# Sixteen value loads moved behind other casts in GpSimd's instruction stream

## The chip, the core and the metric

One NeuronCore of a Trainium2 chip runs the whole program. The engines named below are TensorE (PE in the profile, its weight loads PEld), VectorE (DVE), ScalarE (ACT), GpSimd (POOL) and SyncE (SP). The metric is the device time of one execution in microseconds (us). The kernel before takes 266.47 us, the median of five runs (266.29 to 267.04).

## What is computed

The first half is attention over 4 batches x 8 heads, 768 positions of 64 values. Each query sees only some blocks of 64 keys: its own block and the 3 blocks whose mean key scores best among those not in the future. The second half is a mixer over the 768 x 512 result: one product over positions, one over channels, each with a residual.

```python
k_rep = k.reshape(B, H, 12, 64, D).mean(axis=3)
gate  = where(causal, einsum('bhsd,bhnd->bhsn', q, k_rep), -1e9)
sel   = top 3 of gate, and the own block
attn  = softmax(where(mask(sel) & causal, q @ k.T / 8, -1e9))
x     = (attn @ v), heads side by side          # (4, 768, 512)
u     = x + (relu(x.T @ w_tok1) @ w_tok2).T     # w_tok1 768x256, w_tok2 256x768
out   = u + relu(u @ w_ch1) @ w_ch2             # w_ch1 512x1536, w_ch2 1536x512
```

Inputs and output are float32; the kernel computes most products in float16.

## The kernel before, in words

**Tiling.** Two heads of one batch are a pair, so there are 16 pairs, numbered 0 to 15, four for each batch. For a pair the kernel does the following. Words in brackets are the names that the profile shows.

- SyncE loads keys and queries as float32, two DMAs each (kl and ql, line 313). Three buffers each exist for kl and ql, so the load of pair i waits for the transposes of pair i-3.
- PE transposes them (tkl, tql, line 358) into one of two large PSUM buffers (ring "big"); ACT copies the result out to SBUF (kt, qt, line 367), which frees the PSUM buffer.
- GpSimd casts kt and qt to float16, one cast for each head (KA, QA, line 374): four casts for a pair. For pair 0 ACT does this instead (line 379).
- DVE sums the key blocks (kst, ks, lines 387 and 395), PE multiplies queries by these sums (gps, line 405), DVE picks the three best blocks (gm, m, bn, lines 447 to 483), PE turns the resulting bias (bps, line 493), and DVE puts it under the queries (QA, line 499), so that the score product adds the mask by itself. From pair 6 on, this gate is made for groups of two or four pairs (gtp, gbp, lines 415 and 435).
- PE makes the scores (sps, lines 513 and 517) in three parts for each head, each in a "big" buffer; ACT takes the exponential (e, line 526); DVE clears the half above the diagonal (line 533; for pair 0 PE does it).
- GpSimd issues the load of the pair's values (V, line 320), one DMA that reads float32 and writes float16. There are six V buffers, so the load of pair i waits for the attention product of pair i-6.
- PE multiplies exponentials and values (avp, line 545), and DVE divides by the sums (rc, x, lines 553 and 564).

When the pairs of a batch are done, the mixer of that batch follows: tok and ups (lines 607 and 621 for batch 0, 576 and 588 for the others), then the two large products (c, lines 657 and 678), and the stores. Their weights come through ten more DMAs that GpSimd issues: two for w (lines 706, 707) and eight for wc (lines 709, 711).

**What sets the order.** A planner (`plan`, line 109) runs when the program is built. It gets a list of operations, each with its engine, an assumed duration, a priority, the operations it depends on and the buffers it takes; for a DMA, `size` is the assumed time of its transfer. It puts each engine's operations in an order, and the kernel emits them in that order. On the chip each engine runs its own stream in order, and a semaphore wait exists only where data or a buffer demands one. A dependency that is given to the planner alone sets the place in the stream and nothing else. So for the value load of pair i the planner is told (line 832) to wait for the query transposes of pair 1, 2, 2, 3, 3, 4, 4, 5, ... ; on the chip the DMA waits for what stands ahead of it on GpSimd, and for its buffer.

The planner also fills time that it believes idle on PE up to 46 us with dummy matmuls (avp<-warm, line 695), 136 of them in this program.

GpSimd's stream before, from the end of its set-up to the first casts of pair 8 (V0 is the value load of pair 0; kt1 means both casts of the keys of pair 1, kt7a and kt7b the single ones; w1, w2, wcA to wcH the weight loads):

```
V0 kt1 qt1 V1 V2 kt2 qt2 kt3 V3 w1 w2 qt3 V4 wcA wcB kt4 V5 qt4 V6 wcC wcD own V7
kt5 qt5 wcE wcF kt6 V8 qt6 kt7a wcG wcH kt7b qt7 V9 V10 kt8 ...
```

Of the kernel before, what the change touches and what calls it, by code (L numbers as in the profile page):

```python
# [28 lines left out]
R = 5  # L29
# [10 lines left out]
def QACT(i):  # L40
    return i < 1


GATE = {2: 700, 3: 700, 4: 730}
GROUPED = [[0], [1], [2], [3], [4], [5], [6, 7], [8, 9, 10, 11], [12, 13, 14, 15]]
WAIT = [("kt", 3, 1), ("kt", 3, 1), ("qt", 3, 1), ("qt", 3, 1), ("qt", 4, 1), ("qt", 4, 1),
        ("qt", 5, 1), ("qt", 5, 1), ("qt", 6, 1), ("qt", 6, 1)]
# [171 lines left out]
def kernel(  # L219
# [71 lines left out]
    def op(eng, occ, rec, deps, prio, fn, takes=(), size=0):  # L291
        o = Op(eng, occ, rec, deps, prio, fn, takes, size)
        ops.append(o)
        return o

    def pe(occ, deps, prio, fn, takes=(), tail=170):
        return op("PE", occ, occ + tail, deps, prio, fn, takes)

    def act(cols, deps, prio, fn, takes=()):
        return op("ACT", 70 + cols * 0.833, 173 + cols * 0.833, deps, prio, fn, takes)  # L300

    def dve(occ, deps, prio, fn, takes=()):
        return op("DVE", occ, occ + 84, deps, prio, fn, takes)


    def load_qk(i, t32, src):
        b, h = pairs[i]

        def f():
            t = sb(t32, [128, NJ, 2 * D], FP, f"{t32}_{i}")  # L310
            T[t32, i] = t
            for g in range(2):
                nc.sync.dma_start(out=t[:, :, D * g:D * g + D], in_=src[b, h + g].rearrange("(j p) d -> p j d", p=128))  # L313
        return f

    def load_v(i):
        b, h = pairs[i]

        def f():
            nc.gpsimd.dma_start(out=V16[i % (R + 1)].rearrange("p g j d -> p (g j) d")[:, :, 0:D],  # L320
                                in_=v[b, h:h + 2].rearrange("g (j p) d -> p (g j) d", p=128))
        return f
# [29 lines left out]
    def transposes(t32, i):  # L352
        def f():
            p = ps("big", None, f"t{t32}")
            T["tr", t32, i] = p
            t = T[t32, i]
            for j in range(NJ):
                nc.tensor.transpose(out=p[:, 128 * j:128 * j + 128], in_=t[:, j, :], identity=ident32)  # L358
        return f

    def evac_t(t32, i):
        def f():
            name = "qt" if t32 == "ql" else "kt"
            t = sb(name, [128, S], FP, f"{name}_{i}")
            T[name, i] = t
            p = T["tr", t32, i]
            nc.scalar.copy(out=t, in_=p[:, 0:S])  # L367
        return f

    def cast(dst, name, i, x):  # L370
        def f():
            lo = 64 * x
            to, src = dst[i % R][x][0:64, :], T[name, i][lo:lo + 64, :]
            nc.gpsimd.tensor_copy(out=to, in_=src)  # L374
        return f

    def cast_act(dst, name, i, x):
        def f():
            nc.scalar.copy(out=dst[i % R][x][0:64, :], in_=T[name, i][64 * x:64 * x + 64, :])
        return f  # L380
# [115 lines left out]
    def put_mask(gi, s, x):  # L496
        def f():
            i = GROUPED[gi][s]
            nc.vector.tensor_copy(out=QA[i % R][x][64:MK, 128:S], in_=T["bps", gi][32 * s:32 * s + 2 * NB, :])  # L499
        return f  # L500
# [197 lines left out]
    O = {}  # L698
# [13 lines left out]
    W = []  # L712

    def prepare(i):
        b, h = pairs[i]
        gi = [n for n, G in enumerate(GROUPED) if i in G][0]
        i0 = GROUPED[gi][0]
        pre = 10.0 * (i0 - (AHEAD if i < FIRST else LATER)) + 2.5 * (i - i0) - (0 if len(GROUPED[gi]) == 1 else EXTRA)
        vpre = 10.0 * (i - (AHEAD if i < FIRST else LATER))
        old = i - R  # L720

        def last_scores(x):
            return [O.get(("sc", old, x, g)) for g in range(3)]

        for t32, src, off in (("kl", k, 0), ("ql", q, 0.1)):
            bf = Buf(t32)
            O[t32, i] = op("SP", 950, 0, [], pre - 12 + off, load_qk(i, t32, src), [bf], size=1750)
            big = Buf("big")
            O["tr", t32, i] = pe(660, [O[t32, i]], pre + off, transposes(t32, i), [big], tail=320)
            bf.users.append(O["tr", t32, i])  # L730
            name = "kt" if t32 == "kl" else "qt"
            tb = Buf(name)
            O[name, i] = act(768, [O["tr", t32, i]],
                             pre + 0.5 + off, evac_t(t32, i), [tb])
            big.users.append(O[name, i])
            dst = KA if name == "kt" else QA
            for x in range(2):
                occ = 770
                if QACT(i):
                    O["cast", name, i, x] = act(768, [O[name, i]] + last_scores(x), pre + 0.9 + 0.2 * x + off, cast_act(dst, name, i, x))  # L740
                    tb.users.append(O["cast", name, i, x])
                    continue
                O["cast", name, i, x] = op("POOL", occ, occ + 55, [O[name, i]] + last_scores(x), pre + 4 + off,
                                           cast(dst, name, i, x))
                tb.users.append(O["cast", name, i, x])
            if name == "kt":
                O["ksum", i] = dve(870, [O["kt", i]], pre + 1, ksum(i))
                tb.users.append(O["ksum", i])
                O["kcopy", i] = dve(200, [O["ksum", i], O.get(("gate", old))], pre + 1, kcopy(i))
            else:  # L750
                qb = tb
        O["v", i] = op("POOL", 1060, 0, [O.get(("av", i - R - 1, x)) for x in range(2)], vpre + 2, load_v(i), size=1350)
        n = len(GROUPED[gi])
        O["qb", i] = qb
        if i == GROUPED[gi][-1]:
            G = GROUPED[gi]
            if n == 1:
                gb = Buf("bank")
                O["gate", i] = gate_op = pe(1120, [O["kcopy", i], O["qt", i]], pre + 2, gate(i), [gb])
            else:  # L760
                tbig = Buf("big")
                gate_op = pe(GATE[n], [O["kcopy", m] for m in G] + [O["qt", m] for m in G], pre + 2, gate_t(gi), [tbig])
                for m in G:
                    O["gate", m] = gate_op
                gtb = Buf("gt")
                ge = act(S - 128, [gate_op], pre + 2.1, gate_e(gi), [gtb])
                tbig.users.append(ge)
                gb = Buf("big")
                gback = pe(550, [ge], pre + 2.2, gate_b(gi), [gb])
                gtb.users.append(gback)  # L770
            for m in G:
                O["qb", m].users.append(gate_op)
            gs = Buf("gs")
            O["gm", gi] = dve(75 + 125 * n, [gate_op] if n == 1 else [gback, own_op], pre + 3, gm(gi), [gs])
            gb.users.append(O["gm", gi])
            tops = [dve(720, [O["gm", gi]], pre + 3, top(gi, s)) if s == 0 else None for s in range(n)]
            for s in range(1, n):
                tops[s] = dve(720, [tops[0]], pre + 3, top(gi, s))
            O["lt", gi] = dve(75 + 125 * n, tops, pre + 3, below(gi))
            O["bias", gi] = dve((75 + 125 * n) if n == 4 else 200 * n, [O["lt", gi], O.get(("mask", gi - NBN))] + ([own_op] if n == 4 else []), pre + 3, bias(gi))  # L780
            gs.users += [O["bias", gi]]
            O["lt", gi].two = O["bias", gi].two = True
            mb = Buf("bank")
            O["mask", gi] = pe(280, [O["bias", gi]], pre + 4, mask(gi), [mb])
            for s, m in enumerate(G):
                for x in range(2):
                    O["put", m, x] = dve(410, [O["mask", gi]] + [O.get(("sc", m - R, x, g)) for g in range(3)],
                                         pre + 4, put_mask(gi, s, x))
                    mb.users.append(O["put", m, x])
# [38 lines left out]
        for i in G:  # L828
            attend(i)

    for i, d in enumerate((1, 2, 2, 3, 3, 4, 4, 5, 6, 7, 8, 9, 10, 11, 12, 13)):
        O["v", i].deps.append(O["tr", "ql", d])
    own_op.deps.append(O["cast", "qt", 4, 1])
    for x in range(2):
        O["cast", "kt", 0, x].deps.append(O["qt", 0])
    O["ksum", 1].deps.append(O["bias", 0])
    for n, (at, f) in enumerate(wq):
        W.append(op("POOL", 700, 0, [O[("cast",) + WAIT[n]]], at, f, size=4500 if n < 2 else 2100))

    for b in range(B):  # L840
        fill = 1000.0 * (b + 1)
# [5 lines left out]
        if b == 0:  # L847
            for c in range(4):
                bk = Buf("bank")
                at = fill + c  # L850
# [133 lines left out]
```

The softmax here doesn't subtract the row's maximum and nothing guards it: scores larger than these inputs give would overflow.

## Time and profile before

| what | us |
|---|---|
| median of five runs | 266.47 |
| the profiled execution, its own time | 266.29 |
| its span, first to last instruction | 264.2 |
| PE busy | 257.2 (97%) |
| DVE busy | 158.4 (60%) |
| ACT busy | 145.1 (55%) |
| GpSimd busy | 80.1 (30%) |

The span is what the profiler's instructions cover; the execution's own time is 2.1 us more. PE's busy time is modelled by the profiler and counts matmuls at half clock as busy. In the table of DMA issues the value loads have the time from issue to landing:

```profile
V<-in_v_dram POOLq DMA_DIRECT2D x16, 192.0 KB, 7.2
wc<-in_moe_w_ch_dram POOLq DMA_DIRECT2D x8, 384.0 KB, 9.8
w<-in_moe_w_tok_dram POOLq DMA_DIRECT2D x2, 384.0 KB, 9.6
```

The columns are the issuing queue, the number of issues, the size of one as written (the reads are twice that, float32), and the median us from issue to landing.

### The profile page before, as it was taken

To read this page: it belongs to the slowest core of one execution; us is meant where nothing else is said; L and a number is where in the kernel's file an instruction comes from. 1 tells how busy PE (TensorE), PEld (TensorE's weight loads), DVE (VectorE), ACT (ScalarE), POOL (GpSimd) and SP (SyncE) were. 2 spreads that over 40 slices of the span, in tenths; PEclk is the share of its full clock that TensorE was granted. 3 is DMA by queue.
4 is the path that set the end of the run, shared out by engine and by line. 5 is a ranking of instruction groups with operands and counts; after the bars stand their busy time and mean duration, and the time that the engine had idled before them with its cause. 6 is when DMAs were issued, how large, how long until landed. Compare 5 with 4: busy or idle time off the path is not lost.

```text
span 264.2 us, 5842 instructions
## 1 busy us (share of the span) xinstructions
PE 257.2 (97%) x2304; PEld 167.7 (63%) x2304; DVE 158.4 (60%) x536; ACT 145.1 (55%) x195; POOL 80.1 (30%) x112
## 2 busy tenths in 40 slices
PE   8989999999999999899999999999999999999994
PEld 7877788886768777455656666654455544465443
DVE  3576869986987669986548975483243253333222
ACT  2855898777788965549873699950034400044000
POOL 8393909849464944226420000000000000000000
PEclk9997999999999999999999999999999999999999
DMA  8999999999999999168511000009220025310032
GB/s 167 207 184 205 173 182 221 184 186 200 199 161 171 202 177 143 40 95 136 72 42 42 0 2 0 2 0 201 79 79 2 0 54 144 122 40 0 2 144 94
DMA packets 91322, 28.77 MB, mean 109 GB/s; under 512 B 84896, under 2 KB 87840, under 8 KB 91296
## 3 DMA queue, kind: packets, MB, share of 16 engines
q1 hardware_dynamic: 63232, 21.33, 38.9%
q0 software_dynamic: 28064, 7.08, 27.1%
q8 instruction: 18, 0.29, 0.5%
q14 instruction: 8, 0.07, 0.1%
HBM read 26.83 MB, written 6.29 MB: 125 GB/s over the span
## 4 chain that ended last, share of the span: by engine, by line
PE 85%; DVE 7%; SPq 2%; DMA 2%; ACT 1%; issue 1%; DVEq 0%; ACTq 0%
PE c L657 24%; PE c L678 23%; PE sps L513 13%; PE avp L545 8%; PE ups L588 3%; PE tql L358 3%; PE tkl L358 3%; DMA kl<-in_k_dram 2%; SPq L313 2%; PE tok L576 2%; DVE m L463 1%; DVE kst L387 1%; PE gtp L415 1%; DVE QA L499 1%; PE gps L405 1%; PE tok L607 1%
## 5 line engine op out<-in xcount | busy, mean ns | idle before, releaser
L526 ACT ACTIVATE e<-sps 128x1024 f16<-128x1024 f32 (+1 forms) x96 | 84.4, 920 | 18.1 <-PE sps L513 14.2
L657 PE MATMUL c<-uT,wc 128*128 128x256 f16 (+1 forms) x384 | 69.1, 326 | 0.0
L678 PE MATMUL c<-wc,h 128*128 128x512 f16 (+2 forms) x300 | 65.6, 370 | 0.0
L667 ACT ACTIVATE h<-c 128x512 f16<-128x512 f32 x48 | 28.7, 599 | 61.1 <-PE c L657 42.8
L513 PE MATMUL sps<-QA,KA 88*128 88x512 f16 (+3 forms) x256 | 51.1, 310 | 0.1
L657 PEld LDWEIGHTS <-wc 128*128 128x128 f16 x384 | 36.5, 97 | 23.0 <-issue 0.2
L678 PEld LDWEIGHTS <-h 128*128 128x128 f16 x300 | 28.7, 98 | 30.6 <-issue 1.0
L533 DVE TENSOR_TENSOR e<-e,m 128x256 f16<-128x256 f16 x90 | 29.4, 335 | 14.8 <-ACT e L526 14.1
L374 POOL CAST KA<-kt 64x768 f16<-64x768 f32 x30 | 24.7, 824 | 44.8 <-ACT kt L367 27.7
L686 DVE TENSOR_TENSOR ob<-u,c 128x512 f32<-128x512 f16 (+2 forms) x25 | 16.5, 664 | 32.2 <-PE c L678 32.1
L669 DVE TENSOR_SCALAR h<-c 128x256 f16<-128x256 f32 x48 | 20.3, 422 | 25.8 <-PE c L657 25.3
L513 PEld LDWEIGHTS <-KA 88*128 88x128 f16 x256 | 23.4, 100 | 17.6 <-issue 1.5
L545 PEld LDWEIGHTS <-e 128*128 128x128 f16 x672 | 25.7, 98 | 2.9 <-issue 0.2
L374 POOL CAST QA<-qt 64x768 f16<-64x768 f32 x30 | 25.6, 853 | 5.7 <-ACT qt L367 4.2
L545 PE MATMUL avp<-V,e 128*128 128x65 f16 x672 | 27.0, 194 | 0.0
L367 ACT COPY kt<-tkl 128x768 f32<-128x768 f32 x16 | 12.8, 799 | 13.0 <-PE tkl L358 8.6
L387 DVE TENSOR_REDUCE kst<-kt 128x12 f32<-128x768 f32 x16 | 15.2, 950 | 6.0 <-ACT kt L367 5.7
L564 DVE TENSOR_TENSOR x<-avp,rc 128x384 f16<-128x384 f32 x32 | 17.8, 555 | 0.8
L320 POOL DMA_DIRECT2D V<-in_v_dram x16 | 16.5, 1035 | 5.5 <-PE avp L545 3.3
L499 DVE COPY QA<-bps 24x640 f16<-24x640 f16 x32 | 14.3, 480 | 1.9 <-PE bps L493 1.6
L358 PE MATMUL tkl<-id,kl 128*128 128x128 f32 x96 | 14.2, 286 | 0.8 <-DMA kl<-in_k_dram 0.8
L367 ACT COPY qt<-tql 128x768 f32<-128x768 f32 x16 | 12.8, 802 | 3.4 <-PE tql L358 3.2
(66 smaller groups left out, 214.1 us busy)
## 6 DMA issues: line engine op xcount, KB each, us to landing
kl<-in_k_dram SPq DMA_DIRECT2D x32, 192.0 KB, 5.5
ql<-in_q_dram SPq DMA_DIRECT2D x32, 192.0 KB, 5.5
out_dram<-ob SPq DMA_DIRECT2D x23, 256.0 KB, 2.0
V<-in_v_dram POOLq DMA_DIRECT2D x16, 192.0 KB, 7.2
wc<-in_moe_w_ch_dram POOLq DMA_DIRECT2D x8, 384.0 KB, 9.8
w<-in_moe_w_tok_dram POOLq DMA_DIRECT2D x2, 384.0 KB, 9.6
out_dram<-ob SPq DMA_DIRECT2D x1, 160.0 KB, 1.8
out_dram<-ob SPq DMA_DIRECT2D x1, 96.0 KB, 1.7
```

The source lines that it names most:

```text
L358: nc.tensor.transpose(out=p[:, 128 * j:128 * j + 128], in_=t[:, j, :], identity=ident32)
L367: nc.scalar.copy(out=t, in_=p[:, 0:S])
L374: nc.gpsimd.tensor_copy(out=to, in_=src)
L387: nc.vector.tensor_reduce(out=kst, in_=kt.rearrange("p (n w) -> p n w", w=64), axis=AX.X, op=ALU.add)
L513: nc.tensor.matmul(out=p[:, off + a:off + a + n], lhsT=KA[i % R][x][0:MK, 128 * kk:128 * kk + 128], rhs=QA[i % R][x][0:MK, q0 + a:q0 + a + ...
L526: nc.scalar.activation(out=e[:, 0:width], in_=T["sps", i, x, g][:, 0:width], func=AF.Exp, scale=scale)
L533: nc.vector.tensor_tensor(out=d, in0=d, in1=m0.rearrange("p (a b) -> p a b", a=1).broadcast_to([128, 2, 128]), op=ALU.mult)
L545: nc.tensor.matmul(out=p[:, jq, :], lhsT=T["e", i, x, g][:, o:o + 128], rhs=V16[i % (R + 1)][:, x, kk, :], start=(kk == 0), stop=(kk == jq))
L657: nc.tensor.matmul(out=p, lhsT=wc1_16[:, cc, 128 * fc:128 * fc + 128], rhs=T["uT", b][:, cc, a // 128:e // 128, :], start=(cc == 0), stop= ...
L667: nc.scalar.activation(out=T["h2", b][:, fc, a:e], in_=T["c1", b, fc, n], func=AF.Relu)
L669: nc.vector.tensor_scalar(out=T["h2", b][:, fc, a:e], in0=T["c1", b, fc, n], scalar1=0.0, scalar2=None, op0=ALU.max)
L678: nc.tensor.matmul(out=T["c2", b, j, lo], lhsT=T["h2", b][:, fc, 128 * j:128 * j + 128], rhs=wc2_16[:, fc, lo:hi], start=(fc == 0), stop=( ...
```

## The change

The planner's dependency of each value load is another one. It was the query transposes of some pair; it is now the second cast of the keys or queries of a pair, from a table VAFTER. The planner's transfer time of the weight loads is split by kind: the first two keep 4500 ns, the next four go from 2100 to 2400, the last four from 2100 to 2800. No instruction is added or taken away on the chip other than dummy matmuls, which are 128 instead of 136.

```diff
+VAFTER = [("kt", 1), ("kt", 2), ("qt", 2), ("qt", 3), ("qt", 3), ("kt", 4), ("qt", 4), ("qt", 5),
+          ("qt", 6), ("qt", 7), ("qt", 8), ("qt", 9), ("qt", 10), ("qt", 11), ("qt", 12), ("qt", 13)]
...
-        O["v", i] = op("POOL", 1060, 0, [O.get(("av", i - R - 1, x)) for x in range(2)], vpre + 2, load_v(i), size=1350)
+        last_av = [O.get(("av", i - R - 1, x)) for x in range(2)]
+        O["v", i] = op("POOL", 1060, 0, last_av, vpre + 2, load_v(i), size=1350)
...
-    for i, d in enumerate((1, 2, 2, 3, 3, 4, 4, 5, 6, 7, 8, 9, 10, 11, 12, 13)):
-        O["v", i].deps.append(O["tr", "ql", d])
+    for i, (name, m) in enumerate(VAFTER):
+        O["v", i].deps.append(O["cast", name, m, 1])
...
-        W.append(op("POOL", 700, 0, [O[("cast",) + WAIT[n]]], at, f, size=4500 if n < 2 else 2100))
+        W.append(op("POOL", 700, 0, [O[("cast",) + WAIT[n]]], at, f, size=4500 if n < 2 else 2400 if n < 6 else 2800))
```

GpSimd's stream after, over the same stretch (qt1a and qt1b are the two casts of the queries of pair 1):

```
kt1 qt1a V0 qt1b kt2 qt2a V1 qt2b V2 kt3 w1 w2 qt3 V3 wcA wcB V4 kt4 V5 qt4 wcC wcD own V6
kt5 qt5 wcE wcF V7 kt6 qt6 kt7a wcG wcH kt7b qt7 V8 V9 kt8 ...
```

Further on, V10 stands behind qt8 and V11 behind qt10, where they stood ahead of kt8 and behind qt8; V12 to V15 keep their places. Since the planner derives every stream anew, those of PE, DVE and ACT change too, up to pair 4's second avp; after that they are the same, and SyncE's stream is the same throughout. On PE four things change:

- Pair 0's second head: the first part of its scores stands directly behind the last part of the first head, and the bias turn of pair 1 (bps) behind its second part instead of ahead of both. The key transposes of pair 3 stand ahead of pair 0's first avp instead of behind it.
- The last score part of pair 1's second head stands behind pair 1's first avp instead of ahead of it, and that of pair 2's first head behind pair 1's second avp.
- The first tok of batch 0 stands ahead of pair 2's first avp instead of behind it, and the third behind pair 5's transposes.
- Of the dummies behind the first bps, 47 are left of 55. The 15 ahead of pair 1's second avp become 2, and 8 stand beside pair 0's scores where 2 stood.

## The prediction

> **What bounds the kernel now.** I read the page's rows by slice first, then the waits, the stretches where something broke the pattern, and the timelines of PE and GpSimd there.
>
> ```profile
> PE   8989999999999999899999999999999999999994
> PEclk9997999999999999999999999999999999999999
> ```
>
> PE is busy nearly throughout, so what ends the kernel is PE's work plus the time it lost. Each slice is 6.6 us; the clock has one hole, in the fourth. The list of waits names PE's largest in the loading stage:
>
> ```profile
> PEld tkl L358 <- ACT qt L367: 1.0, 1, 1.0
> PE tkl L358 <- DMA kl<-in_k_dram: 0.8, 1, 0.8
> PE bps L493 <- DVE bn L483: 0.3, 1, 0.3
> ```
>
> The columns are total us, times, longest us. A table of stretches of equal length shows the hole (us of the stretch, then busy time of PE, PEld, DVE, ACT, POOL with instruction counts, the granted clock, the DMA share, GB/s):
>
> ```profile
> 13.10:16.50 3.40, 2.87 (x33) 2.74 (x33) 2.52 (x6) 1.85 (x3) 3.22 (x5) 1.00 1.36 221
> 16.50:19.90 3.40, 3.06 (x30) 2.58 (x30) 2.42 (x16) 2.16 (x3) 3.24 (x5) 0.99 1.28 148
> 19.90:23.20 3.30, 3.30 (x27) 2.26 (x26) 2.15 (x14) 1.59 (x3) 1.36 (x2) 0.50 1.74 178
> ```
>
> For 3.3 us the clock is half. Work done there would have taken 1.65 us. From PE's timeline (start, length, what):
>
> ```profile
> 13.63 0.85 PE L358 MATMUL tkl<-id,kl 128*128 128x128 f32 x6 [0.84 <-DMA kl<-in_k_dram]
> ...
> 19.74 0.65 PE L493 MATMUL bps<-id,bn 128*32 128x128 f16 x5 [0.34 <-DVE bn L483]
> ...
> 22.63 1.11 PE L545 MATMUL avp<-V,e 128*128 128x65 f16 x21
> ```
>
> And from GpSimd's timeline, the value loads among the casts:
>
> ```profile
> 7.01 1.18 POOL L320 DMA_DIRECT2D V<-in_v_dram  x1
> 12.34 1.70 POOL L374 CAST KA<-kt 64x768 f16<-64x768 f32 x2 [4.15 <-ACT kt L367]
> 14.10 1.71 POOL L374 CAST QA<-qt 64x768 f16<-64x768 f32 x2
> 15.76 2.02 POOL L320 DMA_DIRECT2D V<-in_v_dram  x2
> ```
>
> From 38 us on PE is busy 10.00 of 10, 13.77 of 14 and 20.00 of 20 us up to 82 us, and its instructions from pair 4's second avp on are unchanged. So the change is worth what PE gains or loses before that, if nothing later takes it back. The gain can't exceed what PE lost there: 0.84 + 0.34 waiting, some 0.4 in smaller gaps, 1.65 of clock, and the 8 dummies taken out (12 of them take 0.64 us on the chain, so 0.4), 3.6 us in all.
>
> **Part 1: V0 leaves the start.** It is issued at 7.01 and lands 6.1 us later, at 13.1. Beside it runs the key load of pair 2, whose halves are issued at 6.76 and 7.76 and take 4.5 and 5.7 us; the second lands at 13.5 and PE waits 0.84 us for it. The key load of pair 0, alone, took 2.8 and 3.4; the query load of pair 1, just before V0, up to 4.6, so SyncE's own queue accounts for most of that. Without V0 the second half should take 4.6 to 5.0: 12.4 to 12.8. But the transposes also wait for ACT's copy of pair 1's queries, which frees their PSUM buffer (12.18 + 0.79 = 12.97; the weight-load row of 1.0 above). So they start at 13.05 instead of 13.63: **0.58 us**. Its bounds: 0 if V0 was not what delayed the load, 0.58 otherwise, no more. The trend speaks for the latter.
>
> What follows shifts with it: the copy of kt (14.57), the queries' transposes, and both gps of pairs 1 and 2, whose block sums are ready at 14.63 and, shifted, at 16.1. Pair 0's first head ends at 18.8 instead of 19.4.
>
> **Part 2: V0 is late instead.** It now stands behind three casts. These can't start before ACT's copy of pair 1's keys (11.49 + 0.79, which waits for ACT's own casts of pair 0), so at 12.34: 1.70 + 0.06 + 0.82, V0 issues at 14.9. What does it take? The Trainium skill (DMA: Bandwidth & Descriptors, the fit for a DMA issued from GpSimd) gives 2.0 us and 436 kB per us, by estimate 2.5 us for its 197 kB, so landing at 17.4. The nearest row is V1, issued at 15.76 amid the same SyncE loads: 5.8 us. I take the row: V0 lands at **20.7 to 21.0**. The same page's rule for overlap, to issue a DMA early and wait late, speaks against the change outright: 7.9 us of early issue are given up. Before, av of pair 0 began 9.5 us after V0 landed; the question is whether it is wanted before 21.
>
> PE after the change, with durations of the rows before: the last score part of head 0 at 18.27, the first of head 1 behind it (0.7) to 19.5, seven dummies, the second part (ACT frees its buffer at 19.6) to 20.4, bps to 20.85 (its bias is ready at 19.1, so the 0.34 us wait is gone), the key transposes of pair 3 (their buffer is freed by the exponential that ends at 20.7) 20.8 to 21.5, then av. So av wants V0 at 21.5, with 0.5 to 0.8 us to spare, and ends at 22.2. Before, the same set of work ended at 24.16 less bps, which came even later (24.75). Gain here: **2.0 us**, of which 0.58 is part 1, 0.34 the bps wait, and the rest the clock.
>
> That rests on **the clock staying full**. The Trainium skill (TensorE: Matmul & The Clock Gate, on oscillation) says that idle gaps over some 3.4 us drop it. PE's longest gap here is 0.84 us, so by the rule there would be no drop, and no 1.65 us to win; the row shows 0.50 nonetheless. What stands ahead of the drop is 4 us of thin work: gps with 24 columns, short score parts, the bps wait. After the change the thin stretch is 15.6 to 18.3, and from there scores and dummies are dense until av. I think it more likely than not that the drop goes, and keep both ends: 0 and 1.65.
>
> **Part 3: the reordered stretch, 22 to 40 us.** Followed on with measured durations:
> - Pair 3's block sums (DVE: mask of pair 2, then a sum of 0.95, then 0.33) let gps start at 25.7, before 27.6; PE waits 0.3 us for it.
> - Pair 1's exponentials start at 25.1 on ACT, before 27.4.
> - av of pair 1 at 29.1, before 31.5; V1, issued at 19.4 behind qt2a, lands at 25 to 27 by the 5.8 and 7.8 of V1 and V2 before.
> - w1 is issued at about 24.4, because kt3 comes 2 us earlier, V3 (1.02) no longer stands ahead, and w1 no longer waits for V3's data. Before: issued 28.03, landed 36.9, 3.9 after V3. Now 31.5 to 33.3. The tok that moved ahead wants it at 33.3: no reserve at the late end, a loss of up to 1 us.
> - ACT is the tight engine here, 8.96 of 10 us busy from 28 to 38. Its six exponentials from 33.38 on start 2.0 earlier, at 31.4, and the relu of tok falls among them (0.4). Pair 4's key transposes wait for their buffer to 36.5, before 38.1: gain 1.65. The last score part of pair 3's first head: 40.45, before 42.67, with the same work behind it: 2.2.
>
> So **2.0 us** of gain where the streams become equal.
>
> **Part 4: does it stay?** GpSimd's casts come up to 1.0 us later behind a moved value load, 30% busy engine, and scores want them 5 us and more after (qt4's cast ends at 44.3, its scores start at 50.35): nothing. V3 to V11 keep over 3 us of reserve: V3, issued near 27.7 behind w1 and w2, lands by 38 (10.2 us, V4's row), wanted at 42.5. DMA is the tighter cover. SyncE issues without a pause from 56.75 to 87, pair 10's keys land at 69.6 + 12.6 = 82.2 and are transposed at 82.75. If PE comes 2 us earlier, so must they. Their start is set by buffers that PE frees earlier too; and V11, issued at 76.4 with reads of 393 kB, now stands behind qt10, so one value load fewer shares the engines before 82, about 1.5 us by V0's effect. I count 0, and up to 1 us of loss as a bound. The weight sizes act on the planner alone: nothing of their own.
>
> **Sum.** 266.29 - 2.0 = 264.3 us for the profiled execution, whose time lies 0.18 under the median of 266.47; I forecast **264.3**, span about 262.2. This case alone: 263.4 (all but 0.7 of the 3.6) to 265.0.
>
> **Rivals.**
> - *The drop of the clock stays or moves.* The thin stretch is shorter but still there. Then only 0.58, 0.34 and the dummies count, some 1.0 us: 265.3.
> - *Given back.* DVE is busy 8.66 of 10 us at 38 to 48 and 12.77 of 14 after; if it or the loads near 82 can't come earlier, PE waits there: 266.2. Against it, their inputs come earlier as well.
> - *V0 comes late to av.* Place: pair 0's first avp, with all of PE behind it. Price: each us beyond 21.5 in full, and up to 1.65 more if the wait brings the clock down. It decides once it has eaten the 2.0, when V0 takes over 8.6 us from its issue. The row next to it says 5.8, V2's 7.8 (behind V1); but loads with heavier company took 10.2 to 12.5. With 10.2 it lands at 25.1: 3.6 - 2.0 = 1.6 us slower, with a part of the clock 268.3.
> - *The change doesn't do what it says.* The DMA has no wait of its own on a cast, but GpSimd's stream runs in order and the casts ahead wait for ACT, so it is held. Counted at nothing.
>
> **Chances.** Forecast 0.50, clock drop stays 0.18, given back 0.12, V0 late 0.20. About 0.2% (0.5 us) is what a measurement can tell from no change. Faster: 0.50 + 0.18 + 0.02 of the third; within: 0.08 of the third and 0.01 of the last; slower: the remaining 0.21. The range 263.3 to 267.0 leaves out some 0.05 below and 0.14 above.
>
> **What would show it.** Right: the value load at 14.9 on GpSimd, tkl of pair 2 at 13.05 with its DMA wait gone, granted clock 1.00 from 19.9 to 23.2, av of pair 0 at 21.5 without a wait on V's DMA, tok without one on w1, tkl of pair 6 near 53.9 (55.87 before). Wrong: a DMA V row among PE's waits; a clock under 1 anywhere from 16 to 30; PE waiting for kl or ql near 80.

## The result and the profile after

The changed kernel takes **264.96 us** (median of 29 executions, 263.23 to 266.25); the kernel before, on the same chips, 266.60 (50 executions, 265.22 to 268.78). The ratio is 0.9929, 95% interval 0.9913 to 0.9946: 0.7% faster, which is 1.9 us of 266.6 (the ratio is one of averages; the medians alone differ by 1.6). The forecast stood 2.0 us under its own reference. In the ratios, here and below, six executions of all kernels together that took over 1.5% more than the fastest of their kernel are left out; the medians keep them.

The profiled execution of the changed kernel is the longest of its 29 (266.25, span 264.2, as long as the span profiled before). So its trace shows both halves of the story: what PE wins early, and how in this execution all of it is lost again. First the rows of PE and of the clock by slice, and the chain by engine:

```profile
PE   7999999989799997999999999999999999999994
PEclk9999999999999999999999999999999999999999
...
PE 89%; DMA 8%; ACT 1%; issue 1%; SPq 0%; DVEq 0%; DVE 0%; ACTq 0%
```

The hole of the fourth slice is gone from the clock. DMA holds 8% of the chain, where before it held 2%:

```profile
PE 85%; DVE 7%; SPq 2%; DMA 2%; ACT 1%; issue 1%; DVEq 0%; ACTq 0%
```

The list of PE's waits says where:

```profile
PE tql L360 <- DMA ql<-in_q_dram: 2.6, 2, 1.4
...
PE tql L360 <- issue: 1.0, 1, 1.0
PE sps L515 <- ACT e L528: 0.6, 2, 0.4
PE tkl L360 <- DMA kl<-in_k_dram: 0.5, 1, 0.5
```

Pair 2's wait for its keys and the wait of bps are off the list; new are two waits for query loads, one for a key load, two short ones for ACT's exponentials, and one ahead of query transposes for which no releaser is shown. The last is a wait for a load too: it stands ahead of pair 7's queries, whose second half is issued at 44.3 and lands 13.3 us later, at 57.6; the transposes begin at 57.72. The three stretches of 3.4, 3.4 and 3.3 us, as before the change:

```profile
13.10:16.50 3.40, 3.40 (x40) 3.15 (x38) 2.84 (x10) 2.52 (x3) 3.23 (x5) 1.00 1.13 199
16.50:19.90 3.40, 3.40 (x39) 2.70 (x38) 2.78 (x23) 2.88 (x4) 3.28 (x4) 1.00 1.48 155
19.90:23.20 3.30, 3.30 (x56) 2.94 (x57) 3.04 (x9) 2.38 (x4) 3.15 (x5) 1.00 1.65 214
```

PE has no gap left here, and 56 matmuls stand where 27 stood at half clock. GpSimd's timeline (start, length, what, idle before), and PE's at the steps that the prediction named, with the late waits:

```profile
11.83 1.71 POOL L376 CAST KA<-kt 64x768 f16<-64x768 f32 x2 [4.77 <-ACT kt L369]
13.59 0.82 POOL L376 CAST QA<-qt 64x768 f16<-64x768 f32 x1
14.37 1.18 POOL L322 DMA_DIRECT2D V<-in_v_dram  x1
```

```profile
12.26 0.83 PE L360 MATMUL tkl<-id,kl 128*128 128x128 f32 x6
...
20.55 0.83 PE L547 MATMUL avp<-V,e 128*128 128x65 f16 x21
...
52.20 0.87 PE L360 MATMUL tkl<-id,kl 128*128 128x128 f32 x6
...
57.72 0.85 PE L360 MATMUL tql<-id,ql 128*128 128x128 f32 x6 [1.04 <-issue]
...
70.75 0.85 PE L360 MATMUL tql<-id,ql 128*128 128x128 f32 x6 [1.39 <-DMA ql<-in_q_dram]
...
101.80 0.84 PE L360 MATMUL tql<-id,ql 128*128 128x128 f32 x6 [1.25 <-DMA ql<-in_q_dram]
...
104.74 0.85 PE L360 MATMUL tkl<-id,kl 128*128 128x128 f32 x6 [0.52 <-DMA kl<-in_k_dram]
```

ACT's copies of pair 1's keys and queries, which free the buffers of their transposes:

```profile
10.97 0.79 ACT L369 COPY kt<-tkl 128x768 f32<-128x768 f32 x1
11.66 0.79 ACT L369 COPY qt<-tql 128x768 f32<-128x768 f32 x1
```

In the kernel before, the keys of pair 6 were transposed here:

```profile
55.87 0.85 PE L358 MATMUL tkl<-id,kl 128*128 128x128 f32 x6
```

Lead of PE over the kernel before, by the start of the same work: keys of pair 2 1.37 us (13.63 before), first avp 2.08 (22.63), keys of pair 6 **3.67** (55.87), keys of pair 8 2.59 (71.08), keys of pair 9 1.13 (80.56), the last key transposes -1.0 (103.74). From 3.67 us ahead to 1.0 behind, PE loses 4.7 us; the four waits for loads are 4.2 of them. The last gtp then starts at 136.67, before at 136.71: between them the kernel before has a wait of 0.7 us for DVE's ob that PE, being later, no longer has.

Where the loads fall behind is seen on SyncE (its queue's timeline: start and time that the two issues of a load take):

```profile
36.25 6.19 SPq L315 DMA_DIRECT2D kl<-in_k_dram  x2
42.54 3.51 SPq L315 DMA_DIRECT2D ql<-in_q_dram  x2
46.14 7.85 SPq L315 DMA_DIRECT2D kl<-in_k_dram  x2
54.09 5.93 SPq L315 DMA_DIRECT2D ql<-in_q_dram  x2
```

These are keys and queries of pairs 7 and 8. The same four before the change:

```profile
38.95 0.96 SPq L313 DMA_DIRECT2D kl<-in_k_dram  x2
41.42 3.92 SPq L313 DMA_DIRECT2D ql<-in_q_dram  x2
48.56 1.08 SPq L313 DMA_DIRECT2D kl<-in_k_dram  x2
49.74 6.25 SPq L313 DMA_DIRECT2D ql<-in_q_dram  x2
```

The first comes 2.7 us earlier, because PE frees its buffer earlier; but the issues get stuck (it begins with the queries of pair 6, whose two issues take 6.50 us from 29.65 on, where they took 1.73), and the queries of pair 8 are issued 4.35 us **later** than before while PE wants them earlier. They land at 70.61 (57.34 + 13.27 in the chain), and PE waits 1.39 us.

### The profile page after: what moved, and what is told of

Its sections match the earlier page's. It is cut to its first block, busy times and chain, and to the rows that moved or that the text cites. A ratio compares the mean times of both kernels' runs of the same rounds, so it can differ in the third digit from the quotient of the medians.

```text
span 264.2 us, 5828 instructions
## 1 busy us (share of the span) xinstructions
PE 254.5 (96%) x2296; PEld 165.5 (63%) x2296; DVE 157.8 (60%) x536; ACT 145.5 (55%) x195; POOL 80.1 (30%) x112
## 4 chain that ended last, share of the span: by engine, by line
PE 89%; DMA 8%; ACT 1%; issue 1%; SPq 0%; DVEq 0%; DVE 0%; ACTq 0%
PE c L680 23%; PE c L659 22%; PE sps L515 13%; PE avp L547 8%; DMA ql<-in_q_dram 5%; PE tkl L360 3%; PE avp L697 3%; PE tql L360 3%; PE ups L590 3%; DMA kl<-in_k_dram 3%; PE gps L407 3%; PE tok L578 2%; PE tok L609 1%; PE ups L623 1%; PE bps L495 1%; PE gtp L417 1%
## 5 line engine op out<-in xcount | busy, mean ns | idle before, releaser
L659 PEld LDWEIGHTS <-wc 128*128 128x128 f16 x384 | 36.5, 97 | 23.0 <-issue 0.2
L515 PE MATMUL sps<-QA,KA 88*128 88x512 f16 (+3 forms) x256 | 50.2, 305 | 0.6 <-ACT e L528 0.6
L322 POOL DMA_DIRECT2D V<-in_v_dram x16 | 16.5, 1030 | 4.4 <-PE avp L547 3.2
L360 PE MATMUL tql<-id,ql 128*128 128x128 f32 x96 | 13.4, 276 | 3.8 <-DMA ql<-in_q_dram 2.6
```

The costliest lines, as they stand in the source:

```text
L515: nc.tensor.matmul(out=p[:, off + a:off + a + n], lhsT=KA[i % R][x][0:MK, 128 * kk:128 * kk + 128], rhs=QA[i % R][x][0:MK, q0 + a:q0 + a + ...
L659: nc.tensor.matmul(out=p, lhsT=wc1_16[:, cc, 128 * fc:128 * fc + 128], rhs=T["uT", b][:, cc, a // 128:e // 128, :], start=(cc == 0), stop= ...
```

## The experiments

Two theories were set against each other. One is the prediction's: the early stretch decides, by the place of V0 and by the clock, and the loads keep up. The rival: PE wins more than that, the DMA engines give part of it back, and V6 to V11 are moved late for their sake.

In most kernels GpSimd's DMAs are moved in the finished list behind a named cast, and everything else is left as planned. In these lists w0 and w1 are the two loads of w, w2 to w9 the eight of wc:

```diff
     order, span = plan(ops, RINGS)
+    order = requeue(order, O, W, ind_op, own_op)
```

Each execution also has its mean granted clock over the span. 3.3 us at half clock out of 264 make 0.994; the runs fall into three groups, at 0.997 and over ("full"), 0.991 to 0.994 (one such stretch) and 0.988 and below (two or more). Only the profiled executions show where in the span a stretch lies. The kernel before ran beside the experiments on three chips; kernels of different chips are best compared by their ratios. Medians in us:

| kernel | median (runs) | ratio to before, 95% | full / one / two | median at full clock |
|---|---|---|---|---|
| before, beside the experiments | 267.09 (138) | 1 | 54 / 57 / 27 | 266.38 |
| the change | 264.96 (29) | 0.9929 (0.9913 to 0.9946) | all full | 265.0 |
| the change, with the experiments | 265.27 (22) | 0.9931 (0.9907 to 0.9955) | 19 / 2 / 1 | 265.05 |
| queue_only | 265.31 (22) | 0.9931 (0.9905 to 0.9957) | 11 / 7 / 4 | 264.44 |
| plan_only | 265.48 (17) | 0.9941 (0.9913 to 0.9969) | 14 / 1 / 2 | 265.18 |
| v0_only | 264.81 (14) | 0.9908 (0.9877 to 0.9939) | 13 / 1 / 0 | 264.80 |
| early_only | 267.18 (22) | 0.9985 (0.9961 to 1.001) | 11 / 11 / 0 | 266.55 |
| half_v | 262.64 (6) | 0.9832 (0.9792 to 0.9872) | all full | 262.64 |
| dummies_before | 266.08 (22) | 0.9972 (0.9949 to 0.9995) | 21 / 1 / 0 | 266.03 |
| no_dummies_after | 265.18 (11) | 0.9931 (0.9897 to 0.9965) | all full | 265.18 |
| v0_and_late | 264.72 (8) | 0.9919 (0.9879 to 0.9958) | 7 / 1 / 0 | 264.67 |
| queue_dummies | 264.71 (6) | 0.9913 (0.9882 to 0.9945) | all full | 264.71 |
| v11_back | 265.71 (21) | 0.9945 (0.9924 to 0.9966) | 18 / 3 / 0 | 265.64 |
| loads_later | 264.09 (6) | 0.9899 (0.9869 to 0.993) | all full | 264.09 |

### Which half of the change: queue_only and plan_only

queue_only keeps the old streams of PE, ACT and DVE and gives GpSimd the change's; plan_only is the reverse.

```diff
+QUEUE = "kt1 qt1a V0 qt1b kt2 qt2a V1 qt2b V2 kt3 w0 w1 qt3 V3 w2 w3 V4 kt4 V5 qt4 w4 w5 own V6 kt5 ..."   # queue_only
+QUEUE = "V0 kt1 qt1 V1 V2 kt2 qt2 kt3 V3 w0 w1 qt3 V4 w2 w3 kt4 V5 qt4 V6 w4 w5 own V7 kt5 ..."           # plan_only
```

> GpSimd's stream of the change, all other streams as before (136 dummies, pair 0's scores, tok and so on in the old places). If the moved loads are what pays: pair 2's key transposes near 12.3 to 13.0 us instead of 13.63, and the clock full from 16 to 30, 1.5 to 2 us faster than before (ratio about 0.993). If the plan's new order on PE is what pays: only 0.6 to 1.0 us faster (0.996 to 0.998), and the stretch of half clock near 20 us stays.

> All streams of the change but GpSimd's, which has the value and weight loads where they were before (V0 first). If PE's order pays: the clock stays full, 1.3 to 2 us faster than before (0.992 to 0.995) although pair 2's keys land at 13.5 again. If the loads pay: within 0.5 us of before, with the key wait of 0.8 back.

Each alone gives nearly the whole gain (0.9931 and 0.9941), so the two don't simply add. They reach it in different ways. plan_only still waits for pair 2's keys (0.77 us, its transposes at 13.68), but runs at full clock in 14 of 17 executions. queue_only has pair 2's keys transposed at 12.67, but bps waits 0.45 us and the clock still falls in half of its executions. In the profiled one a single hole of about 3.4 us lies across two stretches in which the change has 1.00 (columns as above):

```profile
16.50:19.90 3.40, 2.95 (x25) 2.13 (x24) 3.09 (x24) 1.73 (x2) 3.22 (x5) 0.85 1.38 141
19.90:23.20 3.30, 3.30 (x38) 2.72 (x37) 1.87 (x9) 2.05 (x2) 2.39 (x3) 0.64 1.64 222
```

So the queue's order removes the key wait, and with the new order of PE the clock holds. That both together give no more than each alone suggests that something behind them caps the gain. At full clock queue_only is no slower than the change (264.44 against 265.05), so the new order on PE shows no worth of its own beyond the clock.

### V0 alone: v0_only

```diff
+QUEUE = "kt1 qt1a V0 qt1b V1 V2 kt2 qt2 kt3 V3 ..."   # the rest as before
```

> The kernel before with one DMA moved: V0 behind the first cast of pair 1's queries. If taking V0 from the start is worth 0.58 us and nothing else: ratio 0.998, half clock near 20 us stays. If the earlier transposes alone fill the thin stretch: clock full, ratio 0.992. If V0 comes late to the first attention product: a wait there after 21 us, ratio 1.000 or more.

One load moved by 7.8 us gives 0.9908, as much as the whole change within the intervals. Its waits on PE include:

```profile
PE avp L567 <- DMA V<-in_v_dram: 0.7, 1, 0.7
PE tql L380 <- DMA ql<-in_q_dram: 0.7, 1, 0.7
```

V0 does come late (first avp at 20.71, 0.7 us waited), and the kernel is faster all the same. Its clock was full in 13 of 14 executions, although PE's stream is that of before. In its profile bps comes at 18.22 with no wait ahead of it, where queue_only waits 0.45 us; but one profile of each doesn't settle why V0 alone keeps the clock and queue_only doesn't. They differ in the places of V1 and the loads after it.

### Do the loads give it back, and are the late moves needed: early_only, v11_back, half_v

early_only is the change with V5 to V11 at their old places (V5's place among the casts is the same in both, so V6 to V11 are what moves); v11_back has V11 alone back behind pair 8's casts. half_v is the change with half of every value load left out.

```diff
+QUEUE = "... V4 kt4 V5 qt4 V6 w4 w5 own V7 kt5 ... kt6 V8 qt6 ... V9 V10 kt8 qt8 V11 kt9 ..."   # early_only
+QUEUE = "... V8 V9 kt8 qt8 V10 V11 kt9 ..."                                                    # v11_back
-  nc.gpsimd.dma_start(out=V16[...].rearrange(...)[:, :, 0:D], in_=v[b, h:h + 2].rearrange(...))
+  nc.gpsimd.dma_start(out=V16[i % (R + 1)][:, 0, :, 0:D], in_=v[b, h].rearrange("(j p) d -> p j d", p=128))   # half_v
```

> The change, but V5 to V11 stand in GpSimd's stream where they stood before; V0 to V4 and all other streams are the change's. If the late moves (V11 at 88 us beside the last key and query loads) cost what the profile of the change loses at 101 and 104 us, this is 0.5 to 1.5 us faster than the change (ratio to before 0.988 to 0.991). If the late moves spare the loads before 72 us, it is 0.5 to 1 us slower than the change (0.995 to 0.997). If neither, as the change (0.993).

> The change with V11 alone where it was, behind qt8. If that one load made the change's late part (265.0 with full clock against 266.6 with V5 to V11 in the old places): 0.5 to 1.5 us slower than the change. If V5 to V9 made it: as the change.

> The change with the loads of every pair's second head's values left out: half the bytes of each value load, all sixteen still issued in the same places (the buffers are set to 1 at the start). If what the change gains by 56 us is given back because key and query loads come late from full DMA engines, the waits for ql and kl after 56 us go and this is 1 to 2 us faster than the change (ratio to before 0.985 to 0.990). If the loss sits elsewhere (PE's order, DVE), it stays within 0.5 us of the change (0.991 to 0.995).

early_only is still 2.15 us ahead of before at the keys of pair 6 (53.72) and loses nearly all of it: 0.9985, and at full clock 1.5 us over the change (1.4 by the ratios), more than the 0.5 to 1 us that was expected for this case. Its list of waits begins:

```profile
PE tkl L382 <- DMA kl<-in_k_dram: 1.8, 1, 1.8
PE tql L382 <- DMA ql<-in_q_dram: 1.4, 2, 0.9
```

The late moves are therefore part of the gain. V11 alone seems to be worth 0.6 us of the 1.5 (265.64 against 265.05 at full clock), but the intervals of the two ratios overlap.

With half the bytes, PE's list has no key or query load on it at all; this is all of it over 0.5 us:

```profile
PE avp L697 <- DVE warm L927: 1.3, 1, 1.3
PE ups L590 <- DVE ob L688: 0.7, 1, 0.7
PE sps L515 <- ACT e L528: 0.6, 2, 0.4
```

and its stretches beside those of the change (first half_v, then the change; PE's busy time is the second number, the DMA share the last but one):

```profile
48.00:62.00 14.00, 14.00 (x164) 10.69 (x162) 12.07 (x41) 11.03 (x15) 10.65 (x14) 1.00 1.23 195
62.00:82.00 20.00, 20.00 (x210) 14.58 (x209) 16.02 (x60) 16.35 (x23) 9.43 (x12) 1.00 1.02 163
```

```profile
48.00:62.00 14.00, 12.96 (x155) 10.10 (x155) 11.96 (x41) 10.08 (x15) 10.82 (x15) 1.00 1.40 185
62.00:82.00 20.00, 18.61 (x197) 13.13 (x196) 13.92 (x55) 15.14 (x21) 7.74 (x9) 1.00 1.27 174
```

PE's instructions are the same, and in these stretches PE never stops. Keys of pair 6 are transposed at 52.47, 3.4 us ahead of before, and the last gtp at 133.18, 3.5 ahead of 136.71: here the lead stays. The median is 262.64 against 265.0 (by the ratios, 0.0097 to 0.0099 or 2.6 us), so **some 2.4 us** is what waiting for the loads costs the changed kernel. On SyncE the keys of pair 8 issue in 1.00 us, not 7.85, and its queries at 45.62, not 54.09:

```profile
44.53 1.00 SPq L315 DMA_DIRECT2D kl<-in_k_dram  x2
45.62 4.32 SPq L315 DMA_DIRECT2D ql<-in_q_dram  x2
```

Not all of the 2.4 us need be new. The kernel before wasn't run with half loads; its profiled execution waits for no load after 14 us and without its hole, if nothing took the time back later, would take 264.64 (266.29 - 1.65), but its median at full clock is 266.38. By this estimate late waits, of loads or others, cost its usual executions over 1 us as well. The edit also shortens what GpSimd spends on each value load (839 ns, 1030 in the change); with GpSimd busy 30% and no wait on its casts in PE's list, that is the weaker explanation, but it wasn't separated.

### The clock: dummies_before, no_dummies_after, queue_dummies

The first puts 8 dummy matmuls into the kernel before, ahead of pair 1's bps; the second takes the 8 of that stretch out of the change; the third is queue_only with the first's dummies.

```diff
+    at = order.index(O["mask", 1])                                                     # dummies_before, queue_dummies
+    order[at:at] = [Op("PE", 0, 0, [], IDLE, dummy(n)) for n in range(8)]
+    lo, hi = order.index(O["sc", 0, 1, 0]), order.index(O["av", 0, 0])                 # no_dummies_after
+    order = [o for n, o in enumerate(order) if not (lo < n < hi and o.prio == IDLE)]
```

> The kernel before with eight more dummy matmuls on PE ahead of pair 1's bias turn, where PE waits 0.34 us; no load moved. If thin work ahead of 20 us is what halves the clock: clock full, 1.0 to 1.6 us faster than before (0.994 to 0.996). If the key wait at 13 us does it: clock still 0.5 near 20 us, time as before or 0.2 us more.

> The change without the eight dummies among pair 0's scores. If they hold the clock up: half clock comes back near 20 us and it is 1 to 1.6 us slower than the change (ratio to before 0.997 to 1.000). If the earlier key transposes and the denser scores do it alone: clock full, as the change or 0.2 us faster.

> All of the change's queue on GpSimd, PE, ACT and DVE in the order of before, and eight dummies ahead of pair 1's bias turn. If the change's two parts (clock held up, loads moved) add up and its order on PE is not needed: clock 0.997 or more throughout, 264.4 us at a before of 267, about 0.5 us faster than the change. If the change's order on PE is worth something of its own, slower than the change.

Eight matmuls take the share of executions below full clock from 84 of 138 (23 of 34 on the same chip) to 1 of 22, and in queue_only from 11 of 22 to none of 6. In dummies_before the clock holds even though this execution waits twice as long for pair 2's keys:

```profile
PE tkl L358 <- DMA kl<-in_k_dram: 1.5, 1, 1.5
```

```profile
16.50:19.90 3.40, 3.40 (x37) 3.10 (x36) 2.49 (x16) 2.08 (x4) 3.23 (x4) 1.00 1.49 166
19.90:23.20 3.30, 3.30 (x51) 2.68 (x49) 3.02 (x18) 2.54 (x3) 0.89 (x2) 1.00 1.75 203
```

So here a wait of 1.5 us at 14 us didn't bring the clock down, and a little filling of the thin stretch behind it holds it up. Thin work alone isn't enough to bring it down either. v0_and_late (below) has PE's order of before and in its profile the same thin stretch, with 30 matmuls in 3.03 us and a wait of 0.37 us ahead of bps, and its clock stays full:

```profile
16.50:19.90 3.40, 3.03 (x30) 2.55 (x30) 2.31 (x14) 2.16 (x3) 3.30 (x5) 1.00 1.45 146
19.90:23.20 3.30, 3.29 (x48) 2.54 (x44) 3.13 (x17) 2.40 (x4) 2.12 (x3) 1.00 1.78 183
```

What else has to come together for the drop is open. The change needs no filling: without its eight dummies it has full clock in all 11 executions. And filling alone isn't the change: 0.9972 (0.7 us, less than the 1.0 to 1.6 expected) against 0.9929. queue_dummies, with the change's queue, the old order on PE and the filling, comes out as expected, 0.6 us of medians under the change on the same chip, though the intervals overlap: the new order on PE isn't needed for the gain.

### Repeated, combined, and one step further: change_again, v0_and_late, loads_later

v0_and_late is v0_only with V5 to V11 at the change's places. loads_later takes queue_dummies and lets six value loads wait longer still:

```diff
+QUEUE = "... V7 kt6 qt6 kt7a w8 w9 kt7b qt7 kt8 qt8 V8 kt9 qt9 V9 kt10 qt10 kt11 qt11 kt12 qt12 V10 V11 V12 V13"
```

> The change itself once more, beside the next three on one chip. Clock 0.997 or more in all executions, ratio to before 0.992 to 0.994; how much of it is the clock follows from the executions of before with a clock of 0.997 or more: against those alone 1.2 to 1.5 us.

> The streams of PE, ACT and DVE as before; on GpSimd V0 behind the first cast of pair 1's queries, V1 to V4 as before, V5 to V11 where the change has them. If the late moves spare the key and query loads of pair 10 and 7, the 0.7 us wait near 83 us that V0 alone has is gone and it is 0.3 to 1 us faster than V0 alone (0.987 to 0.990). If they only shift it to the loads of pairs 14 and 15, as V0 alone (0.991).

> As the last one, with V8 behind qt8, V9 behind qt9, V10 to V13 behind qt12. If full DMA engines before 105 us set what is left, the key and query waits go and it comes 1 to 2 us nearer to the 262.6 us of the half loads. If the value loads then come late to pairs 8 to 11 or to the weights, PE waits for V after 110 us and it is slower than the change.

The change repeats (0.9931), though its clock is full in 19 of 22 executions and not in all, as was expected. Its second profile (266.90) waits 0.37 us for V0, and late in the stage mostly where the first does: 1.45 us ahead of the queries of pair 7 (again with no releaser shown), 1.21 for the queries of pair 8, 1.39 for the keys of pair 15. Only the wait for the queries of pair 14 isn't repeated. v0_and_late can't be told from v0_only; its profile lacks the wait for pair 10's queries that v0_only has at 83.23.

loads_later has the lowest median of the kernels that compute everything, 264.09, and is faster than before by 0.7 to 1.3%. Its interval overlaps the change's, so that it beats the change, by 1.2 us of medians on the same chip, is likely rather than shown. It starts from queue_dummies, and is 0.6 us under that, less than the 1 to 2 us expected, again with overlapping intervals. Its list of waits has no key and no query load left:

```profile
PE ups L610 <- DVE ob L708: 0.7, 1, 0.7
PE gps L427 <- DVE ks L417: 0.2, 1, 0.2
PE avp L567 <- DMA V<-in_v_dram: 0.2, 1, 0.2
```

## Why the prediction was right, and where its sum was not

The direction and the means were right (V0 moved away from pair 2's keys, the clock held up), and the size came out: 1.9 us by the ratio for 2.0 forecast. That the size agrees is in part luck, for two terms of the sum are wrong and cancel: PE's early lead was forecast too small, and the late loss at nothing.

- **Part 1, V0 leaves the start: right, too small.** Its wait went. The 0.58 us was capped at the end of ACT's copy of pair 1's queries, 12.97, with "no more". That cap was wrong. Of the two "big" buffers these transposes take the one that the copy of pair 1's *keys* frees. In the changed kernel that copy ends at 11.76; they begin at 12.26, while the copy of the queries runs to 12.45 (ACT's lines above). The weight-load row "PEld tkl <- ACT qt" had been misread: before the change that copy was over at 12.97, and the weights were loaded at 13.60, when the keys had landed, so that wait was the DMA's. In the kernels with V0 moved that were profiled the transposes began at 12.20 to 12.76, so 0.9 to 1.4 us were won.
- **Part 2, V0 at av: mechanism right, reserve too large.** V0 was issued at 14.37 and landed 6.1 us later, at 20.5; the row next to it said 5.8, and the estimate of 2.5 would have been far off. That PE itself would be at av by 20.5, not 21.5, follows from part 1: the reserve of 0.5 to 0.8 us was 0.1, and 0.37 us of waiting in the second profile. The rival of V0 coming late was near, but its price was small: at 0.7 us (v0_only) a wait there costs less than V0 costs at the start. The Trainium skill's rule to issue a DMA early (DMA: Bandwidth & Descriptors, rules for kernel authors) would have kept the kernel before; the measurement decides against it here.
- **The clock: step right, worth mis-sized.** It stayed full in all executions of the first series and in 19 of 22 later. The 1.65 us is what the hole takes at its place; by mean clock only 61% of the executions before have one or more. On the median it is 0.7 (267.09 against 266.38); the other 1.35 (266.38 to 265.0) is won by executions at full clock as well: by these medians most of the gain isn't the clock. The rival "the drop stays" did not come; what it would have looked like is seen in queue_only's executions with one or two stretches at half clock (266.18 and 267.14 against 264.44).
- **Part 3: the lead where the streams become equal was forecast at 2.0 and is 2.9 to 3.7** (keys of pair 6 at 52.20 in the change's first profile, 52.96 in its second, 52.47 in half_v). In the first profile 0.95 us of the excess is part 1's and stands before this stretch begins, with the first avp at 20.55 and not 21.5. The step that failed in the stretch itself is ACT as the tight engine, which was to hold pair 4's keys to 36.5. They were transposed at 35.30, right behind the tok at 34.63, with no wait on ACT there (PE's two waits for exponentials, at 30.30 and 32.13, are 0.42 and 0.16 us); the exponentials that were to start at 31.4 start at 29.54. tok found its weights (issued 23.54) at 32.58. The upper bound of 3.6, worked out from what PE had lost, is about what was reached at this place.
- **Part 4, "I count 0, and up to 1 us of loss as a bound": the term that failed.** Waiting for the loads costs the changed kernel 2.4 us, by half_v; against the usual executions of the kernel before, which seem to lose some time late as well, the loss is smaller, and how much wasn't measured. It was looked for at pair 10 near 82 us alone; it comes at pairs 7 and 8 first, because SyncE's issues get stuck from 30 us on, and at 101 to 105. The rival "given back" named the mechanism, but priced it as all or nothing. That V11 moved later relieves the loads fits: without the moves of V6 to V11 1.5 us more is lost (V11's own share, 0.6, isn't clear of noise).
- **The weight sizes by kind** were counted at nothing of their own. With the old size the planner gives every engine the same stream as the change has, so there is nothing of them to measure.

Against the list of what would show it: the clock at 1.00 and the key wait gone came true, and so did the sign of the wrong, PE waiting for queries and keys late in the stage. What stays open is whether the faster executions lose their lead at the same pairs (both profiles of the change are of executions slower than its median), and where in the span the executions at 0.994 other than the profiled ones lose their clock.

## What to carry to other kernels

When PE is the bound but its loads share DMA engines that are busy nearly all the time, a gain ahead of the loading stage is worth only what the loads can follow: PE's lead of 2.9 to 3.7 us paid 1.9 at the end. Ask of a load not only how early it can be issued but whom it delays; here loads that weren't urgent, held back to about when they are needed, let the urgent ones through. And cost the slack of the next loads at the new speed, with the time that their issue takes under pressure, not at the old starts.

## What the runs showed of the hardware

- **The clock falls without a long gap, and not in every execution.** By the mean granted clock, the same program has one stretch of about 3.3 us at half clock in 57 of 138 executions, two or more in 27, and none in 54. In the profile it follows some 4 us of thin work with no gap over 0.84 us; a like stretch in v0_and_late, behind a gap of 0.93 us, left the clock full, and so did a gap of 1.54 us with 8 dummies behind it. The Trainium skill (TensorE: Matmul & The Clock Gate, on oscillation) speaks of idle gaps over some 3.4 us, which no profile here shows at that place; what makes thin work enough was not measured. 1.65 us of lost work at its place cost 0.8 at the end (266.38 against 267.16), which would fit loads that limit PE later in any case, but this was not tried.
- **Loaded DMA engines show in the issuing queue.** The two issues of pair 8's keys took 1.08 us before the change, 7.85 after it, and 1.00 with half the value bytes. From issue to landing the queries took 9.1 to 13.3 us at 50 to 75 us of the change, and 5.9 to 9.7 with half the value bytes.
